# A step table for gated linear attention is written anew: order, engines and buffers' homes

## The chip, the cores and the metric

The kernel runs on one core of one Trainium2 chip. Its time is the device time of one execution in microseconds, and it is given as the median of several runs. Besides the runs there is one profiled execution, from which all rows below come. A core has a matrix engine (TensorE, PE), three engines for elementwise work (DVE, ACT and GpSimd, which the profile calls POOL), and a queue of its own (SP) from which this kernel issues all its transfers.

## The reference, cut to what matters

There are 8 batches `b`, 8 heads of 64 channels, 576 tokens and 512 channels in all.

```
q_s = softmax of q over the head's channels,   k_s = softmax of k over the tokens
kv  = einsum('bhsd,bhse->bhde', k_s, v)
x   = einsum('bhsd,bhde->bhse', q_s, kv)          # (b, 576, 512) when heads are joined
gate_pre = sum over k < 5 of conv_w[k] * x shifted by 4 - k tokens
gate = 1 / (1 + exp(-gate_pre))
val  = x @ w_val                                  # 512 x 512
out  = (gate * val) @ w_out                       # 512 x 512
```

## The kernel before

Channels lie on the partitions, in 4 blocks of 128, and tokens along the rows. So `x_b_p` is block `p` of batch `b`, 128 x 576, and the two big products, `value b m` and `project b n`, each make one block of an output from the 4 blocks of their input.

The program is a list of some 970 steps, `ORDER`. Each step is a function of the kernel with its arguments, and a last letter tells the engine where there is a choice (a is ACT, v is DVE, p is GpSimd). The steps are issued one after the other, and every engine works through its own instructions in that order. No scheduler changes it. An engine stands still when its next instruction must wait for another engine, for a transfer, or for a buffer.

Buffers come from pools with a fixed number of tiles to a tag, which are handed out in turn. A tile is reused when its last reader is done. There are 4 banks of PSUM for the results of TensorE (`bank`), 6 tiles for `gate`, 6 for staged inputs (`f`), 6 for the pairs of rounded x and its rest (`pair`), 2 for `far`, and 2 each for k, q, v, g and o.

What happens to one batch, by the names of the steps:

- `load_q`, `load_k`, `load_kc`, `load_km`, `load_qc`, `load_v`, `load_vt`, `load_kt`, `load_words` and `put` are transfers. SP issues them in the order of the list, and a load waits there until its buffer is free.
- For batches 0 and 1 q and k are worked out early and by hand: `q_max`, `q_sub`, `q_exp`, `q_each` (eight small exponentials of ACT), `q_sum`, `q_eps`, `q_rec` and `q_mul` make the softmax of q; `k_top` and `k_raise` exponentiate k by channels, and `k_turn` and `k_tail_turn` turn it on TensorE, from where `k_turned` and `k_tail_turned` copy it. `q_turn`, `tail_turn` and their copies (`q_turned`, `tail_turned`, `tail_high`) do the same for q.
- For later batches `k_peak`, `k_row`, `k_spread` and `k_sub` bring the maxima of k to its rows, and `q_total`, `q_log`, `l_turn`, `l_row`, `l_spread`, `l_sub` and `c_exp` turn the sums of q into a subtraction ahead of the exponential.
- `kv b` multiplies k and v, `kv_sums` and `kv_norm` divide by the sums, and `attend b g` makes two blocks of x, each in a bank of its own.
- `x_high` rounds a block of x, `x_low` takes the rest (on DVE), and `value` multiplies both with the rounded `w_val` and its rest: 24 products of two halves in three passes (high with low weights, high with high, low with high).
- The gate of a block starts with `first` (one tap), and 4 more follow, each either as `tap` on DVE or as `far` on ACT and `near` on GpSimd. `sigmoid` is a tanh on ACT, `gated` joins gate and val on DVE, `g_high` and `g_low` split the result, `project` multiplies it with `w_out` in the same three passes, `copy` brings a block of out to SBUF and `put` stores it.
- Blocks 0 and 1 of batch 0 take another way (`diag`, `conv_rows`, `conv_kv`, `conv`, `conv_gate`): their taps are done on TensorE.
- `field`, `part`, `scaled`, `signed` and `joined` decode a slab of weights from pairs of words, `w_high` and `w_low` split it. `taps` does the same in one step for the 20 numbers of the conv weights that each partition needs.

Every reader of `x_b_p` (`x_high`, `first`, `x_low`, `tap`, `far`) keeps its bank from the next product that shall have it.

## Time and profile before

| | |
|---|---|
| median of 3 runs | 288.62 us (288.42 to 288.87) |
| span of the profiled execution | 287.3 us |
| TensorE busy | 267.8 us, 93% of the span |
| DVE busy | 231.5 us, 81% |
| GpSimd busy | 206.2 us, 72% |
| ACT busy | 191.6 us, 67% |
| moved by DMA | 62.92 MB, 219 GB/s in the mean |

The profiled execution has a span of 287.3 us beside the 288.62 us of the median; the runs' times take in what lies around the span. Busy time is the time in which an engine has an instruction at work. Loads of weights into TensorE (PEld) run beside its products. Products are pipelined, so that one may be shown to begin before the one ahead has ended.

### The profile page before, as it was taken

How to read it: one execution, taken by the hardware profiler on the slowest of the kernel's cores; microseconds unless marked ns; L12 is line 12 of the kernel's file. 1: busy time of each engine (PE TensorE's matmuls, PEld its weight loads, DVE VectorE, ACT ScalarE, POOL GpSimd, SP SyncE). 2: the span in 40 equal slices, each digit the busy share in tenths (PEclk: the TensorE clock that was granted, in tenths of full speed). 3: DMA queues.
4: the chain of work that ended last, by engine and by line, in shares of the span. 5: the costliest groups of instructions: out<-in, count | busy, mean ns of one | idle time of the engine just before them, and what ended most of it. 6: DMA issues, size and time to landing. Idle time of an engine off the chain costs nothing.

```text
span 287.3 us, 6606 instructions
## 1 busy us (share of the span) xinstructions
PE 267.8 (93%) x2616; PEld 248.2 (86%) x2616; DVE 231.5 (81%) x332; ACT 191.6 (67%) x323; POOL 206.2 (72%) x187
## 2 busy tenths in 40 slices
PE   0198999999999999999999999999999999999995
PEld 0075799889998899889999898999989898989995
DVE  2999899999979999899669989799659774759610
ACT  2799999977797668856956773688945733645002
POOL 3767968989999986899898993879379193533300
PEclk9999999999999999999999999999999999999999
DMA  7999894598379899969997969645645700112022
GB/s 232 385 412 417 329 332 114 190 332 322 117 164 285 298 259 346 349 223 233 368 411 246 235 232 343 256 164 131 178 149 149 217 8 2 43 41 82 2 82 82
DMA packets 23462, 62.92 MB, mean 219 GB/s; under 512 B 3432, under 2 KB 3976, under 8 KB 20744
## 3 DMA queue, kind: packets, MB, share of 16 engines
q1 hardware_dynamic: 23432, 62.51, 65.5%
q8 instruction: 20, 0.33, 0.5%
q14 instruction: 10, 0.08, 0.1%
HBM read 52.96 MB, written 9.54 MB: 218 GB/s over the span
## 4 chain that ended last, share of the span: by engine, by line
PE 65%; DVE 13%; DMA 8%; POOL 6%; ACT 4%; issue 3%; SPq 0%; DVEq 0%; POOLq 0%; ACTq 0%
PE out_a L593 31%; PE val L593 25%; PE x L543 4%; DMA kc<-in_k_channels 4%; PE kv L484 3%; DMA kt<-in_k_tail 3%; POOL gl L660 2%; DVE gate L568 2%; DVE ktop L339 1%; ACT q L469 1%; DMA words<-in_w_val 1%; POOL q L471 1%; DVE g L652 1%; DVE e L263 1%; DVE qs L393 1%
## 5 line engine op out<-in xcount | busy, mean ns | idle before, releaser
L593 PE MATMUL val<-x,w_val_hi 128*128 128x288 f32 x512 | 89.0, 295 | 0.0
L568 DVE SCALAR_TENSOR_TENSOR gate<-x,cw,gate 128x575 f32<-128x575 f32 (+3 forms) x98 | 78.3, 808 | 4.8 <-ACT gate L556 1.9
L593 PEld LDWEIGHTS val<-x,w_val_hi 128*128 128x128 f32 x512 | 75.2, 188 | 0.1
L593 PE MATMUL val<-x,w_val_lo 128*128 128x288 f32 x256 | 56.0, 300 | 0.1
L593 PE MATMUL out_a<-gh,w_out_lo 128*128 128x288 f32 x248 | 54.6, 301 | 0.2 <-ACT far L573 0.2
L593 PE MATMUL out_a<-gh,w_out_hi 128*128 128x288 f32 x248 | 53.2, 296 | 0.0
L660 POOL TENSOR_TENSOR gl<-g,gh 128x576 fp32r<-128x576 f32 x25 | 36.1, 1443 | 13.8 <-ACT gh L168 6.5
L593 PEld LDWEIGHTS out_a<-gh,w_out_lo 128*128 128x128 f32 x248 | 39.3, 188 | 5.7 <-issue 2.2
L593 PE MATMUL out_a<-gl,w_out_hi 128*128 128x288 f32 x248 | 43.1, 295 | 0.3 <-POOL gl L660 0.3
L593 PEld LDWEIGHTS val<-x,w_val_lo 128*128 128x128 f32 x256 | 40.7, 188 | 1.4 <-issue 0.6
L577 POOL TENSOR_TENSOR gate<-gate,far 128x572 f32<-128x572 f32 (+3 forms) x22 | 29.0, 1320 | 16.4 <-DVE gate L568 8.1
L593 PEld LDWEIGHTS out_a<-gh,w_out_hi 128*128 128x128 f32 x248 | 39.8, 188 | 0.0
L383 POOL TENSOR_TENSOR q<-q,qm 128x512 f32<-128x512 f32 x32 | 32.9, 1044 | 6.3 <-DVE qm L378 6.3
L593 PEld LDWEIGHTS out_a<-gl,w_out_hi 128*128 128x128 f32 x248 | 36.4, 188 | 0.6 <-POOL gl L660 0.6
L174 ACT ACTIVATE o<-out_a 128x576 f32<-128x576 f32 x26 | 16.9, 651 | 29.3 <-PE out_a L593 22.6
L652 DVE SCALAR_TENSOR_TENSOR g<-gate,val 128x576 f32<-128x576 f32 x32 | 23.9, 750 | 15.4 <-PE val L593 10.1
L453 POOL TENSOR_TENSOR qc<-qc,lb 128x576 f32<-128x576 f32 (+1 forms) x17 | 24.3, 1439 | 10.8 <-DMA lb<-lrow 8.2
L318 POOL TENSOR_TENSOR k<-k,kmax 128x512 f32<-128x512 f32 x23 | 30.1, 1328 | 0.2
L580 ACT ACTIVATE gate<-gate 128x576 f32<-128x576 f32 x30 | 20.1, 682 | 8.6 <-DVE gate L568 7.1
L563 DVE TENSOR_TENSOR x<-x,x 128x576 fp32r<-128x576 f32 x32 | 23.2, 749 | 1.7 <-ACT x L168 1.6
L573 ACT ACTIVATE far<-x,cw 128x572 f32<-128x572 f32 (+3 forms) x22 | 16.2, 739 | 12.5 <-PE x L543 4.7
L168 ACT CAST x<-x 128x576 fp32r<-128x576 f32 x27 | 17.0, 640 | 7.3 <-PE x L543 4.2
(110 smaller groups left out, 441.2 us busy)
## 6 DMA issues: line engine op xcount, KB each, us to landing
out<-o SPq DMA_DIRECT2D x31, 288.0 KB, 3.9
v<-in_v SPq DMA_DIRECT2D x8, 1040.0 KB, 8.7
q<-in_q SPq DMA_DIRECT2D x7, 1024.0 KB, 8.6
km<-in_k_strided SPq DMA_DIRECT2D x24, 288.0 KB, 5.5
k<-in_k SPq DMA_DIRECT2D x6, 1024.0 KB, 8.5
qc<-in_q_channels SPq DMA_DIRECT2D x16, 288.0 KB, 7.7
lb<-lrow SPq DMA_DIRECT2D x8, 576.0 KB, 5.9
kc<-in_k_channels SPq DMA_DIRECT2D x8, 288.0 KB, 6.9
```

The lines of the kernel that those rows point to most:

```text
L168: nc.scalar.copy(out=out, in_=in_)
L174: nc.scalar.mul(out, in_, factor)
L318: engine(e).tensor_sub(kk[r, cs], kk[r, cs], mx[r, cs])
L383: engine(e).tensor_tensor(qq, qq, m, op=ALU.add if b < 2 else ALU.subtract)
L453: engine(e).tensor_sub(t, t, T["lb", b][:, p])
L563: nc.vector.tensor_sub(xl, T["x", b, p], T["xh", b, p].bitcast(F32))
L568: nc.vector.scalar_tensor_tensor(out=a, in0=x, scalar=w, in1=a, op0=ALU.mult, op1=ALU.add)
L577: nc.gpsimd.tensor_add(a, a, T["far", b, p, j])
L580: nc.scalar.activation(T["gate", b, p], T["gate", b, p], AF.Tanh, scale=0.5)
L593: nc.tensor.matmul(ps[:, cs], a[:, kb, ms], z[:, cs], start=(i == 0), stop=(i == len(parts) - 1))
L652: nc.vector.scalar_tensor_tensor(out=T["g", b, m], in0=T["gate", b, m], scalar=1.0, in1=T["val", b, m], op0=ALU.add, op1=ALU.mult)
L660: engine(e).tensor_sub(T["gl", b, m], T["g", b, m], T["gh", b, m].bitcast(F32))
```

## The change

The list of steps is another one: nearly all the same steps, in another order on all queues, 77 of them on another engine. GpSimd gives work to DVE (`g_low`, `l_sub`, `k_sub` and copies above all), and some goes between ACT and the two. `taps` becomes five steps, of which `tap_part` is now on ACT and `tap_joined` on GpSimd, so that the list grows from 967 to 971. The tags keep their number of tiles, but which tile a buffer gets is now read from a table, `HOMES`, one digit for each buffer in the order of the list.

```diff
-STAGED = 6
...
-    load_words 3, load_q 0 2 5, field 3 p, load_q 0 1 2, scaled 3 a, signed 3, load_taps, load_words 0, part 3 p,
...
+HOMES = {
+    "pair": "01234501230125340125013401250134012501",
+    "gate": "0123450213412305412305413250142035142031",
...
+    "bank": (
+        "012302302130120120102301302132101012312310202103030321302032121023021310321213201010321212102310"
+        "10213123120303012320320132"
+    ),
...
+    places = {tag: iter(order) for tag, order in HOMES.items()}
+
+    def home(pool, shape, dtype, tag, name):
+        return pool.tile(shape, dtype, tag=f"{tag}{next(places[tag])}", name=name, bufs=1)
 
     def bank(name):
-        return psum.tile([P, 2 * 512], F32, tag="bank", name=name)
-
-    def block(tag, name, bufs, dtype=F32, n=S):
-        return work.tile([P, S], dtype, tag=tag, name=name, bufs=bufs)[:, :n]
-
-    def pair(name, dtype, tag="pair", bufs=6):
-        return work.tile([P, 2 * S], dtype, tag=tag, name=name, bufs=bufs)
+        return home(psum, [P, 2 * 512], F32, "bank", name)
+
+    def block(tag, name, dtype=F32, n=S):
+        return home(work, [P, S], dtype, tag, name)[:, :n]
+
+    def pair(name, dtype, tag="pair"):
+        return home(work, [P, 2 * S], dtype, tag, name)
...
-    def taps():
-
-        w = tap_words.rearrange("p (n t) -> p n t", t=2)
-        lo, hi, e, f = w[:, :, 0].bitcast(U32), w[:, :, 1], tap_parts[:, 0], tap_parts[:, 1].bitcast(I32)
-        nc.vector.tensor_scalar(e, hi.bitcast(F32), MOST, -MOST, op0=ALU.min, op1=ALU.max)
-        nc.vector.tensor_scalar_mul(f, lo, 2.0 ** -29)
-        nc.vector.tensor_scalar_mul(e, e, 2.0 ** -112)
-        e = e.bitcast(I32)
+    def tap_field(e):
+        hi = tap_words.rearrange("p (n t) -> p n t", t=2)[:, :, 1]
+        engine(e).tensor_scalar(tap_parts[:, 0], hi.bitcast(F32), MOST, -MOST, op0=ALU.min, op1=ALU.max)
+
+    def tap_part(e):
+        lo = tap_words.rearrange("p (n t) -> p n t", t=2)[:, :, 0].bitcast(U32)
+        times(e, tap_parts[:, 1].bitcast(I32), lo, 2.0 ** -29)
+
+    def tap_scaled(e):
+        times(e, tap_parts[:, 0], tap_parts[:, 0], 2.0 ** -112)
+
+    def tap_signed():
+        hi = tap_words.rearrange("p (n t) -> p n t", t=2)[:, :, 1]
+        e = tap_parts[:, 0].bitcast(I32)
         nc.vector.tensor_scalar(e, e, 3, None, op0=ALU.logical_shift_left)
         nc.vector.scalar_tensor_tensor(e, hi, -(1 << 31), e, op0=ALU.bitwise_and, op1=ALU.bitwise_or)
-        nc.vector.tensor_add(cw_bits, e, f)
+
+    def tap_joined(e):
+        engine(e).tensor_add(cw_bits, tap_parts[:, 0].bitcast(I32), tap_parts[:, 1].bitcast(I32))
```

Three places show how the instructions move. In the rows a name with a number is a tile, `<-` stands between what is written and what is read, and the shape is that of the result.

The first place is the start of DVE's queue, before. `e` and `words` belong to the weights, `qm` are the maxima of q, `tap_words` the conv weights as they arrive and `tap_parts` their two parts, `cw` the decoded conv weights.

```order
L262 TENSOR_SCALAR e_100<-e_100 128x512
L263 SCALAR_TENSOR_TENSOR e_100<-words_95,e_100 128x512
L378 TENSOR_REDUCE qm_111<-q_97 128x8
L378 TENSOR_REDUCE qm_111<-q_97 128x16
L275 TENSOR_SCALAR tap_parts<-tap_words 128x20
L276 TENSOR_SCALAR tap_parts<-tap_words 128x20
L277 TENSOR_SCALAR tap_parts<-tap_parts 128x20
L279 TENSOR_SCALAR tap_parts<-tap_parts 128x20
L280 SCALAR_TENSOR_TENSOR tap_parts<-tap_words,tap_parts 128x20
L281 ISA cw<-tap_parts 128x40
```

And the same start of DVE's queue in the changed kernel.

```order
L302 TENSOR_SCALAR tap_parts<-tap_words 128x20
L208 TENSOR_SCALAR tap_parts<-tap_parts 128x20
L314 TENSOR_SCALAR tap_parts<-tap_parts 128x20
L315 SCALAR_TENSOR_TENSOR tap_parts<-tap_words,tap_parts 128x20
L291 TENSOR_SCALAR e_99<-e_99 128x512
L292 SCALAR_TENSOR_TENSOR e_99<-words_95,e_99 128x512
L415 TENSOR_REDUCE qm_115<-q_106 128x8
L415 TENSOR_REDUCE qm_115<-q_106 128x16
```

The decoding of the conv weights has gone ahead of the first slab of weights and of the maxima of q, and two of its six instructions have left DVE.

The second place is ACT's queue ahead of the first rounding of x (the last two rows), before. `qs` are the sums of q, `f` a part of the weights, `qT` the turned q, `qTt` its tail, `qTps` the banks that it is copied from, `x_0_1` the rounded block 1 of batch 0.

```order
L398 ACTIVATE qs_152<-qs_152 128x16
L174 ACTIVATE f_233<-words_107 128x512
L469 ACTIVATE q_97<-q_97,qs_152 128x64 x8
L168 COPY qT_252<-qTt_250 128x4x64
L174 ACTIVATE f_305<-words_144 128x512
L174 ACTIVATE f_328<-words_215 128x512
L168 COPY qT_252<-qTps_0_296 128x2x512
L168 COPY qT_252<-qTps_1_317 128x2x512
L168 CAST x_0_1_353<-x_1_342 128x576
L168 CAST x_0_0_355<-x_0_341 128x576
```

And ACT's queue ahead of the first rounding of x in the changed kernel, where `k`, `kps` and `ktz` belong to the turned k.

```order
L198 COPY k_214<-kps_1_153 128x4x256
L198 COPY ktz_83<-ktps_222 64x512
L204 ACTIVATE f_235<-words_189 128x512
L506 ACTIVATE q_106<-q_106,qs_171 128x64 x8
L198 COPY qTt_248<-qTtps_228 128x512
L204 ACTIVATE e_253<-e_253 128x512
L198 COPY qT_321<-qTt_248 128x4x64
L198 COPY qT_321<-qTps_0_301 128x2x512
L198 COPY qT_321<-qTps_1_310 128x2x512
L198 CAST w_val_hi<-f_235 128x4x128
L198 CAST x_0_1_356<-x_1_325 128x576
L198 CAST x_0_0_372<-x_0_324 128x576
```

Two parts of weights have left the stretch, and a copy of the tail of q, a scaling and the rounding of one slab of weights have come into it.

The third place is DVE's queue in the sixth batch, ahead of `attend 6 1`, before. `gate` rows are taps of blocks 0 and 1 of batch 6 (they read `x_0` or `x_1`), `x_6_0` is the `x_low` of block 0, `qc` a subtraction of batch 7 or 6, `lse` and `lt` the `l_turn` of batch 7.

```order
L170 CAST gh_3_2928<-g_3_2926 128x576
L423 TENSOR_TENSOR lse_82<-qm_2626,qs_2778 128x4x8
L428 STREAM_TRANSPOSE lt_2932<-lse_82 32x32 x4
L568 SCALAR_TENSOR_TENSOR gate_1_2970<-x_1_2917,cw,gate_1_2970 128x575
L453 TENSOR_TENSOR qc_2_2906<-qc_2_2906,lb_2710 128x576
L568 SCALAR_TENSOR_TENSOR gate_0_2976<-x_0_2916,cw,gate_0_2976 128x575
L568 SCALAR_TENSOR_TENSOR gate_0_2976<-x_0_2916,cw,gate_0_2976 128x574
L568 SCALAR_TENSOR_TENSOR gate_0_2976<-x_0_2916,cw,gate_0_2976 128x573
L563 TENSOR_TENSOR x_6_0_2972<-x_0_2916,x_6_0_2972 128x576
L568 SCALAR_TENSOR_TENSOR gate_1_2970<-x_1_2917,cw,gate_1_2970 128x574
L568 SCALAR_TENSOR_TENSOR gate_1_2970<-x_1_2917,cw,gate_1_2970 128x573
L568 SCALAR_TENSOR_TENSOR gate_1_2970<-x_1_2917,cw,gate_1_2970 128x572
```

And the same place of DVE's queue in the changed kernel, where `gl` is a `g_low` of batch 5 and `k` two `k_sub` of batch 7.

```order
L697 TENSOR_TENSOR gl_2_2914<-g_2_2871,gh_2_2912 128x576
L595 TENSOR_SCALAR gate_1_2929<-x_1_2920,cw 128x576
L605 SCALAR_TENSOR_TENSOR gate_0_2931<-x_0_2919,cw,gate_0_2931 128x574
L605 SCALAR_TENSOR_TENSOR gate_1_2929<-x_1_2920,cw,gate_1_2929 128x575
L605 SCALAR_TENSOR_TENSOR gate_1_2929<-x_1_2920,cw,gate_1_2929 128x572
L605 SCALAR_TENSOR_TENSOR gate_1_2929<-x_1_2920,cw,gate_1_2929 128x573
L605 SCALAR_TENSOR_TENSOR gate_1_2929<-x_1_2920,cw,gate_1_2929 128x574
L490 TENSOR_TENSOR qc_2_2677<-qc_2_2677,lb_2671 128x576
L605 SCALAR_TENSOR_TENSOR gate_0_2931<-x_0_2919,cw,gate_0_2931 128x575
L600 TENSOR_TENSOR x_6_0_2935<-x_0_2919,x_6_0_2935 128x576
L355 TENSOR_TENSOR k_2518<-k_2518,kmax_2882 128x512 x2
L605 SCALAR_TENSOR_TENSOR gate_0_2931<-x_0_2919,cw,gate_0_2931 128x573
```

A `g_low`, a `first`, two `k_sub` and one tap more have come into the stretch, a rounding and the `l_turn` have left it, and the last reader of `x_0`'s bank is now the last row, behind all of these.

## Rows read from the trace of the kernel before

**Rows 1.** The page, part 1: busy us (share of the span) and instructions.

```profile
PE 267.8 (93%) x2616; PEld 248.2 (86%) x2616; DVE 231.5 (81%) x332; ACT 191.6 (67%) x323; POOL 206.2 (72%) x187
```

**Rows 2.** Windows: length, busy time of each engine, clock, DMA share, GB/s.

```profile
core 0: us, PE busy (x) PEld busy (x) DVE busy (x) ACT busy (x) POOL busy (x), PEclk, DMA share, GB/s
...
2.00:25.00 23.00, 10.25 (x128) 8.11 (x128) 18.90 (x34) 16.61 (x45) 13.53 (x16) 1.00 1.01 380
...
34.00:54.00 20.00, 19.70 (x212) 18.79 (x210) 19.32 (x29) 19.21 (x48) 16.40 (x18) 1.00 0.61 188
...
95.00:103.00 8.00, 7.79 (x65) 6.93 (x66) 7.89 (x12) 6.29 (x9) 6.45 (x6) 1.00 0.84 266
...
119.00:135.00 16.00, 15.68 (x131) 14.26 (x123) 15.78 (x25) 9.47 (x15) 15.35 (x14) 1.00 0.85 249
135.00:284.00 149.00, 149.00 (x1407) 141.69 (x1405) 107.98 (x155) 85.29 (x120) 93.27 (x76) 1.00 0.50 166
```

**Rows 3.** Waits of TensorE: us in total, times, longest.

```profile
PE out_a L593 <- POOL gl L660: 0.3, 1, 0.3
PE out_a L593 <- ACT far L573: 0.2, 1, 0.2
```

**Rows 4.** Timelines, DVE and TensorE from 27 to 50: start, us, instruction.

```profile
27.01 1.42 DVE L563 TENSOR_TENSOR x<-x,x 128x576 fp32r<-128x576 f32 x2
...
32.74 0.75 DVE L563 TENSOR_TENSOR x<-x,x 128x576 fp32r<-128x576 f32 x1
...
33.64 0.37 PE L593 MATMUL val<-x,w_val_lo 128*128 128x288 f32 x1
...
49.48 1.09 PE L509 MATMUL qTps<-ident,q 128*128 128x128 f32 x8
```

**Rows 5.** Timeline of ACT at the end.

```profile
284.13 0.41 ACT L174 ACTIVATE o<-out_l 128x288 f32<-128x288 f32 x1 [1.12 <-PE out_l L593]
```

**Rows 6.** Timeline of ACT from 8 to 27.

```profile
8.59 2.02 ACT L462 ACTIVATE q<-q,qm 128x64 f32<-128x64 f32 x8 [2.94 <-DVE qm L378]
10.51 1.13 ACT L387 ACTIVATE q<-q 128x512 f32<-128x512 f32 x2
...
12.63 1.43 ACT L343 ACTIVATE kc<-kc,ktop 128x576 f32<-128x576 f32 x2
...
26.34 1.18 ACT L168 CAST x<-x 128x576 fp32r<-128x576 f32 x2 [0.42 <-PE x L543]
```

**Rows 7.** Timelines of POOL and DVE from 4 to 10.

```profile
4.35 0.63 POOL L253 TENSOR_SCALAR e<-words 128x512 f32<-128x512 f32 x1 [2.34 <-DMA words<-in_w_val]
...
5.68 0.43 DVE L262 TENSOR_SCALAR e<-e 128x512 int32<-128x512 int32 x1 [5.68 <-ACT e L174]
...
6.75 1.80 DVE L378 TENSOR_REDUCE qm<-q 128x8 f32<-128x512 f32 x2
...
8.68 1.03 DVE L277 TENSOR_SCALAR tap_parts<-tap_parts 128x20 f32<-128x20 f32 x1
```

**Rows 8.** Timeline of POOL from 32 to 34.

```profile
32.73 2.53 POOL L291 TENSOR_TENSOR w_val_lo<-f,w_val_hi 128x512 fp32r<-128x512 f32 x2
```

**Rows 9.** DMA issues: times, KB each, median us to landing.

```profile
v<-in_v SPq DMA_DIRECT2D x8, 1040.0 KB, 8.7
```

**Rows 10.** Timelines of DVE and TensorE from 178 to 224.

```profile
178.38 0.45 DVE L170 CAST gh<-g 128x576 fp32r<-128x576 f32 x1
...
203.16 0.75 DVE L652 SCALAR_TENSOR_TENSOR g<-gate,val 128x576 f32<-128x576 f32 x1
203.83 0.75 DVE L660 TENSOR_TENSOR gl<-g,gh 128x576 fp32r<-128x576 f32 x1
...
212.28 0.75 DVE L652 SCALAR_TENSOR_TENSOR g<-gate,val 128x576 f32<-128x576 f32 x1 [1.84 <-PE val L593]
...
223.00 1.20 PE L543 MATMUL x<-qT,kvd 64*64 64x288 f32 x16
```

**Rows 11.** Timeline of DVE and POOL at 266.

```profile
266.40 1.43 POOL L660 TENSOR_TENSOR gl<-g,gh 128x576 fp32r<-128x576 f32 x1
266.48 1.97 DVE L660 TENSOR_TENSOR gl<-g,gh 128x576 fp32r<-128x576 f32 x1 [0.77 <-POOL gh L170]
```

## Prediction: what the change does to the time

> **What bounds the kernel now.** I start with the page. TensorE is busy for 267.8 of the 287.3 us [rows 1], far more than any other engine, so I ask only where it is idle: that is 19.5 us. The windows give the place: from 2 to 25 us it lacks 12.75, from 34 to 54 0.30, from 95 to 103 0.21, from 119 to 135 0.32, and from 135 to 284 nothing, at a granted clock of 1.00 throughout [rows 2]; the rest is the first two and the last three microseconds. The waits name what it waited for in the middle: a product with `w_out` waited 0.3 for a `gl` of GpSimd and another 0.2 for a `far` of ACT [rows 3]. From `value 0 1` at 33.64 [rows 4] to the last product at 284.1 TensorE is a full pipe of 250.5 us. The last piece costs 0.41 for its copy [rows 5] and then its transfer, some 3.2 us in all. A different order can therefore do three things: move the 33.64, remove the 0.8 of small waits, or make new ones. The TensorE rows themselves hardly change: the same products, with the same 23 returns from a narrow product (`kv`, `attend`, `q_turn`) to a full one.
>
> The profiled execution has 287.3 us beside a median of 288.62 for the runs, so 1.3 lie around the span. I make the sum against 287.3 and carry it to 288.62.
>
> **The start.** In the kernel before, `value 0 1` waits for the DVE queue: `x_low 0 1` starts at 27.01 when ACT has rounded x, then come `x_low 0 0`, a `q_max`, four taps and `x_low 0 3`, which frees the bank at 33.49 (32.74 and 0.75), and TensorE goes on at 33.64 [rows 4]. The same seven instructions stand there in the changed order, so this piece stays 6.63 us long (33.64 less 27.01). What moves is ACT's `x_high 0 1`, at 26.34 now [rows 6]. I add up ACT's queue in the new order. An ACT instruction starts about 0.1 before the end of the one ahead, so I take differences of starts where rows have them.
>
> DVE first decodes the taps. Their words come second in the queue, right behind those that are used at 4.35; I take 4.4, and 5.0 as the other end. The tap steps cost 0.1, 1.03 (the one at 8.68, the longest of them) and 0.42, the sign steps of words 3 1.07 (5.68 to 6.75), two `q_max` 1.72: 4.4 + 4.34 = 8.8 [rows 7]. ACT's first `q_each` so starts at 8.8, 0.2 later than now (8.59). From there: `q_each` 1.92 (8.59 to 10.51), two `q_exp` 1.03, three `k_raise` at 0.68, `q_exp` 0.53, `q_each` 1.91: 16.2. The fourth `k_raise` waits for its maximum, which DVE has at about 16.55 because the block now lands as late as the vt block before: 17.25. `scaled` 0.52, `q_eps` 0.12, `k_turned` 0.90: 18.8; `k_tail_turned` can start at 18.9 and takes 0.47, `part` 0.63, `q_mul` 1.93: 21.9; `tail_turned` 0.47 (moved here from DVE), `scaled` 0.52, `tail_high` 0.29, two `q_turned` 1.80, `w_high 1` 0.52: 25.5 [rows 6]. Two parts, one scaling and a rounding step have come or gone, and the waits of this queue, as the 0.42 ahead of `x_high 0 1`, are gone. `x_high 0 1` starts at 25.5 instead of 26.34, `x_low 0 1` at 26.15, `value 0 1` at 26.15 + 6.63 = 32.8.
>
> GpSimd's `w_low 1` must be there too. It stands behind words 5, about 8.2 MB into the queue; at 380 GB/s from 2 us [rows 2] and 1.5 to 2 us more that is 25.1 to 25.6. Behind it come a `field`, a `w_high` and a `q_sub` (some 2.3), and two `joined` and two `w_low` at 1.26 [rows 8], together 7.3: 32.4 to 32.9. It does not take the lead by much. So 33.64 becomes 32.8 to 33.3; I take **-0.8**, with 0 as one end (taps late by 0.6) and -0.9 as the other.
>
> `load_v 1` now stands behind `load_km 3 0`, which waits for the `k_peak 2 3` behind `gated 0 0`, at 41 to 42 by the same sums. `kv 1` takes the place of a `q_turn` that starts at 49.48 [rows 4], so TensorE wants v at 48.7. A v load lands 8.7 us after its issue in the median [rows 9], which would be late by 1.0 to 2.0; but the queue is at 0.61 in this stretch and at 1.01 before [rows 2], so that I take 0, with 2.0 as the other end.
>
> **The middle.** The 0.21 came from an ACT `far` and the 0.32 from a GpSimd `g_low` [rows 3]. In the new order `project 1 1` takes the bank in question 1.3 us after its last reader by my count, and `g_high 2 2` is on DVE, where a cast of this kind takes 0.45 [rows 10], ahead of an idle GpSimd. I let both go: **-0.5**.
>
> The new wait that I find is `attend 6 1`. The homes put `x_6_3` into the bank of `x_6_0`, whose last reader is now `tap 6 0 1`. DVE does far more ahead of it. From the end of `value 5 0` to that of `value 5 3` TensorE needs 9.1 (`gated 5 0` at 203.16 and `gated 5 3` at 212.28 stand right behind their products). By the distances between starts in its timeline DVE has there `gated` 0.7, `q_total` 2.2, `kv_sums` and `kv_norm` 0.8, `g_high` 0.4, `g_low` 0.76, three `l_sub` 2.1, a tap 0.82, `gated` 0.7, `l_turn` 1.15: 9.6. Then, from `gated 5 3` on, TensorE needs 10.7 to `attend 6 1` (212.28 to 223.00), and DVE has `gated` 0.7, `g_low` 0.76, `first` 0.81, seven taps 5.7, `l_sub` 0.7, `x_low` 0.66, two `k_sub` 1.2: 10.5 [rows 10]. Together 20.1 of work against 19.8 less the 0.3 by which a `gated` starts behind its product. That is 0.6, and with 0.15 from a last reader to the product (33.49 to 33.64) TensorE stands still for about **+0.7**, with 0 and 1.2 as ends. Before, DVE was the one that waited here (1.84 ahead of `gated 5 3`), so nothing stood still.
>
> Elsewhere the added work on DVE (some 9 us in the whole kernel) lies in its idle time: it is busy for 108 of the 149 us from 135 to 284 [rows 2]. GpSimd loses about 19 us and waits for nobody at the end. The last pieces are swapped so that a put of 288 KB, not of 144, goes ahead of the last one; I take 0.
>
> **Sum.** -0.8 - 0.5 + 0.7 = -0.6: 286.7 in the profile, 288.0 as a median.
>
> **Rivals.** *No wait at `attend 6 1`*: if DVE keeps up there, 288.62 - 1.3 = 287.3. For it speaks that I used durations of a DVE that is often waiting.
>
> *The start stays where it is*: the tap words are a small transfer of short rows and may land at 5.0 or later; each 0.1 goes straight through to `q_each` and the whole ACT queue. Then the small gain and the new wait cancel: 288.62 - 0.5 + 0.7 = 288.8. That the new homes do nothing by themselves belongs here, since each group has as many buffers as before.
>
> *DVE and GpSimd block each other* (the slower one). One `g_low` on DVE took 1.97 instead of the 0.75 of another [rows 10], while a GpSimd `g_low` ran from 266.40 to 267.83 [rows 11]: a block costs 1.2. Instructions of DVE with two SBUF inputs (`g_low`, `l_sub`, `k_sub`) grow from 11 to 24, nine of them in the two stretches ahead of `attend 6 1`, where no room is left, so that every block there goes to the end. Two blocks give 288.0 + 2.4 = 290.4, one gives 289.2; one decides. Against it: of the 11 now, only that one shows a full block, and GpSimd has less to do.
>
> By the Trainium skill ("SBUF — State Buffer", section "Who interferes with whom") a DVE instruction with two SBUF inputs and a GpSimd instruction that reads SBUF exclude each other for a whole instruction, whichever came first; the 1.97 agrees, and by that rule any overlap among the nine would cost one of the two engines its wait.
>
> **Chances.** The forecast has 0.46, with a range of its own of 287.6 to 288.5; no wait 0.14; the start unmoved 0.17; blocks 0.23. A run can be told from no change beyond 0.2%, 0.58 us: below 288.04 or above 289.20. Of the forecast two thirds lie below 288.04, and all of the no-wait case: faster 0.46. The rest of the forecast, nearly all of the unmoved start and a little of the blocks: same 0.32. Slower 0.22. For 8 in 10 I go from 287.2 to 289.4, which leaves out the two-block case and the late `v 1` on top of it.
>
> **What would show it.** In the changed profile ACT's first `x_high` near 25.5, `val` from 32.8 on, no TensorE wait from 54 to 200, and then one of about 0.7 ahead of an `x` product near 222. Wrong would be: an `x_high` after 26, a TensorE wait on DVE of more than 1 us, `gl`, `qc` or `k` rows of DVE well above 0.76, or a wait of `kv 1` for v.

## The result: 1% slower, where the prediction expected a little faster

The changed kernel takes 291.52 us in the median of 4 runs (290.4 to 294.37), against 288.62 before: a ratio of 1.0105 (1.0062 to 1.0147). That is outside the predicted range of 287.2 to 289.4 and on the other side of no change. The profiled execution has a span of 288.6 us and a time of its own of 290.4, so it is the fastest of the four; what the other three have on top can be told only in part, below, from other executions of the same kernel. One thing to know for what follows: in every run on record the time lies 1.7 to 1.9 us above the span. The profile of before, with its span of 287.3, is thus of an execution of about 289.1 and not of one at the median. The two profiles lie 1.3 apart, the two medians 2.9.

The page of the changed kernel, part 1, shows what [rows 1] shows of before.

```profile
PE 267.7 (93%) x2616; PEld 247.8 (86%) x2616; DVE 242.0 (84%) x347; ACT 190.9 (66%) x320; POOL 191.1 (66%) x175
```

TensorE does the same 267.7 us of work. DVE has 10.5 more, GpSimd 15.1 less. The windows of [rows 2], with one more from 103 to 119, tell where TensorE now stands still.

```profile
2.00:25.00 23.00, 9.81 (x128) 7.80 (x128) 17.90 (x30) 16.39 (x43) 16.89 (x19) 1.00 0.98 372
34.00:54.00 20.00, 19.77 (x216) 19.20 (x220) 19.79 (x31) 19.52 (x45) 16.49 (x17) 1.00 0.68 248
95.00:103.00 8.00, 7.97 (x66) 6.95 (x65) 7.79 (x12) 5.56 (x9) 7.82 (x7) 1.00 0.76 213
103.00:119.00 16.00, 14.90 (x171) 14.66 (x172) 13.70 (x18) 11.64 (x15) 13.29 (x12) 1.00 0.92 289
119.00:135.00 16.00, 15.69 (x130) 13.88 (x129) 14.01 (x23) 10.77 (x17) 12.68 (x11) 1.00 0.57 181
135.00:284.00 149.00, 149.00 (x1406) 141.59 (x1405) 121.77 (x178) 82.99 (x115) 77.79 (x63) 1.00 0.55 167
```

In the new window it lacks 1.10 us. The waits of TensorE (us in total, times, longest) name the releaser. They answer to [rows 3].

```profile
PE kps L387 <- ACT kc L380: 14.9, 1, 14.9
PE val L630 <- ACT o L204: 1.1, 1, 1.1
...
PE out_a L630 <- POOL gl L697: 0.3, 1, 0.3
```

The wait for a `far` of ACT is gone, the one for a `gl` of GpSimd is still 0.3, and a `val` product now waits 1.1 for a copy of ACT. To see what each place does to the end, I compare the start of the same product in both traces. The changed one is late by 0.24 at `value 0 1` (33.88 against 33.64). It is early by 0.37 at the first `attend` of batch 1 (53.77 against 54.14): most of that is won between `value 0 1` and `k_turn 1 0`, where it takes 6.48 and before took 6.95, with a named wait of 0.2 for DVE. It loses 0.53 at `attend 2 0`, whose weights need a copy of ACT; the product behind it starts 1.66 later, where before it was 1.13:

```profile
86.20 0.39 ACT L198 COPY qT<-qTt 128x256 f32<-128x256 f32 x1
...
86.10 1.73 PE L580 MATMUL x<-qT,kvd 64*64 64x288 f32 x16
```

Before:

```profile
86.33 1.20 PE L543 MATMUL x<-qT,kvd 64*64 64x288 f32 x16
```

It is late by 0.29 at `attend 2 1` (95.18 against 94.89), wins 0.47 where before waited for a `far`, and loses 1.29 at `value 2 1`: there it is late by 1.11 (104.10 against 102.99). Behind that little is added: it is late by 1.21 at the `attend` at 119.78, by 1.29 at `attend 6 1` (224.29 against 223.00) and by 1.37 at the last copy (285.50 against 284.13 in [rows 5]). So in its fastest execution the largest loss is at one place, `value 2 1`, a second one is at `attend 2 0`, and what is won elsewhere, about 1.1, pays for that one and for the late start. These are ACT's timeline ahead of `value 2 1` and the product that waited.

```profile
97.88 0.76 ACT L593 ACTIVATE gate<-x,cw 128x576 f32<-128x576 f32 x1
99.97 0.64 ACT L198 CAST x<-x 128x576 fp32r<-128x576 f32 x1 [1.33 <-DVE gate L605]
100.51 0.41 ACT L198 COPY qT<-qTt 128x256 f32<-128x256 f32 x1
100.92 1.28 ACT L363 ACT_TABLE_LOAD   x1
102.22 0.63 ACT L363 ACTIVATE ktz<-kt 64x512 f32<-64x512 f32 x1
102.86 0.64 ACT L198 CAST x<-x 128x576 fp32r<-128x576 f32 x1
103.39 0.66 ACT L204 ACTIVATE o<-out_a 128x576 f32<-128x576 f32 x1
...
104.10 0.53 PE L630 MATMUL val<-x,w_val_lo 128*128 128x288 f32 x2 [1.14 <-ACT o L204]
```

`value 2 1` needs the bank of `project 1 2`, whose reader is `copy 1 2`, the ACTIVATE at 103.39. ACT was idle until 99.97, because `x_high 2 2` stands behind `tap 2 2 2` of DVE in the list and both read the bank of `x_2_2`. Then come a loading of ACT's function tables for 1.28 and `kt_exp 3`, which needs it, ahead of the copy. In the kernel before the copy stands ahead of the same load:

```profile
100.06 0.66 ACT L174 ACTIVATE o<-out_a 128x576 f32<-128x576 f32 x1
100.74 1.28 ACT L326 ACT_TABLE_LOAD   x1
```

The tap itself is late. Ahead of it on DVE stands the first step of `l_turn 3`, which took 0.20 before (at 94.64) and takes 0.93 here, beside a `k_sub` of GpSimd:

```profile
96.55 0.93 DVE L460 TENSOR_TENSOR lse<-qm,qs 128x32 f32<-128x32 f32 x1
...
96.11 1.29 POOL L355 TENSOR_TENSOR k<-k,kmax 128x512 f32<-128x512 f32 x1
```

An estimate from these rows: with 0.20 there, tap, cast and copy would come some 0.7 earlier, and about 0.4 of the 1.14 would be left. No run moves that step alone, so this share is not shown.

That one reader of a PSUM bank waits for another is not in the kernel's text, but in neither trace does a read of a block of x by ACT overlap with one of the same block by DVE. The Trainium skill ("PSUM — Partial Sum Buffer", section "PSUM bank collisions raise a hardware error ⚠️") says that two engines may not access one bank at the same time, reads included, and that the compiler puts a dependency between them. The 1.33, idle until the tap ended, agrees.

The start, by DVE's timeline (it answers to [rows 7]), one row of ACT ([rows 6]) and one of TensorE ([rows 4]):

```profile
4.72 0.54 DVE L302 TENSOR_SCALAR tap_parts<-tap_words 128x20 f32<-128x20 f32 x1 [4.72 <-DMA tap_words<-in_conv_w]
...
6.38 0.69 DVE L292 SCALAR_TENSOR_TENSOR e<-words,e 128x512 int32<-128x512 int32 x1
7.89 2.50 DVE L415 TENSOR_REDUCE qm<-q 128x8 f32<-128x512 f32 x3 [0.81 <-DMA q<-in_q]
...
26.57 1.73 ACT L198 CAST x<-x 128x576 fp32r<-128x576 f32 x3
...
33.88 0.50 PE L630 MATMUL val<-x,w_val_lo 128*128 128x288 f32 x2
```

The taps are decoded nearly as early as I had put it (4.72 against 4.4). But then DVE waits 0.81 for q, and everything from there is late: `q_each` starts at 9.83, not at 8.8, and `x_high 0 1` at 26.57, not at 25.5.

The place of the predicted new wait, in the timelines of DVE and TensorE ([rows 10] of before):

```profile
223.07 0.81 DVE L605 SCALAR_TENSOR_TENSOR gate<-x,cw,gate 128x573 f32<-128x573 f32 x1
...
224.29 1.20 PE L580 MATMUL x<-qT,kvd 64*64 64x288 f32 x16
```

The tap ends at 223.88 and the product starts 0.41 later, behind its own predecessor on TensorE. No wait stands there.

### The profile page after: what moved, and what is told of

Its sections match the earlier page's. It is cut to its first block, busy times and chain, and to the rows that moved or that the text cites. A ratio compares the mean times of both kernels' runs of the same rounds, so it can differ in the third digit from the quotient of the medians.

```text
span 288.6 us, 6590 instructions
## 1 busy us (share of the span) xinstructions
PE 267.7 (93%) x2616; PEld 247.8 (86%) x2616; DVE 242.0 (84%) x347; ACT 190.9 (66%) x320; POOL 191.1 (66%) x175
## 4 chain that ended last, share of the span: by engine, by line
PE 72%; DVE 12%; ACT 9%; issue 3%; DMA 2%; POOL 1%; SPq 0%; DVEq 0%; POOLq 0%
PE out_a L630 30%; PE val L630 28%; PE kv L521 5%; PE x L580 5%; DVE gate L605 4%; DMA q<-in_q 2%; ACT kc L380 1%; ACT q L506 1%; DVE x L600 1%; ACT qT L198 1%; PE kps L387 1%; PE qTps L546 1%; DVE qm L415 1%; DVE g L689 1%; POOL gl L697 1%
## 5 line engine op out<-in xcount | busy, mean ns | idle before, releaser
L697 POOL TENSOR_TENSOR gl<-g,gh 128x576 fp32r<-128x576 f32 x20 | 29.3, 1469 | 13.7 <-ACT gh L198 8.0
L204 ACT ACTIVATE o<-out_a 128x576 f32<-128x576 f32 x23 | 15.0, 651 | 22.2 <-PE out_a L630 16.5
L355 POOL TENSOR_TENSOR k<-k,kmax 128x512 f32<-128x512 f32 x21 | 27.4, 1320 | 0.1
L198 ACT CAST x<-x 128x576 fp32r<-128x576 f32 x28 | 17.6, 645 | 9.5 <-PE x L580 4.9
L415 DVE TENSOR_REDUCE qm<-q 128x8 f32<-128x512 f32 (+3 forms) x12 | 20.9, 1746 | 0.8 <-DMA q<-in_q 0.8
```

The lines of the kernel that those rows point to most:

```text
L198: nc.scalar.copy(out=out, in_=in_)
L355: engine(e).tensor_sub(kk[r, cs], kk[r, cs], mx[r, cs])
L415: nc.vector.tensor_reduce(out=T["qm", b][:, cs], in_=qq, axis=AX.X, op=ALU.max, negate=b < 2)
L697: engine(e).tensor_sub(T["gl", b, m], T["g", b, m], T["gh", b, m].bitcast(F32))
```

## The experiments

All runs of the kernel before that stand beside these have medians from 288.41 to 289.15. After each kernel I give its median, the lowest and highest run and their number, and the ratio to the kernel before with its interval where it matters. In the edits each step stands on the list as shown, and the dots are steps that stay.

### The same kernel again

No edit. The first repetition was made to see whether the 1.1 is always there, the second to have the change in the same group of runs as the mended versions at the end.

> The changed kernel as it is, to see how far its runs lie apart (290.4 to 294.37 in the first four) and what a second profile shows. All theories: a median near 291.5 us. If v 1 is what varies (theory V: load_v 1 stands behind load_km 3 0, is issued at 42.38 and has its last packet at 48.23, with kv 1 at 49.09), a profile of a longer run has kv 1 waiting at about 49 and the same distances elsewhere. If the start varies (theory S: the words of the taps and then of q land at other times), the first val moves and kv 1 with it. If the middle varies (theory M), everything up to 95 us agrees with the first profile.

Measured: 292.39 us (290.74 to 292.88, 5 runs), ratio 1.0135 (1.0114 to 1.0155). The wait at `value 2 1` is there, 1.1 at 104.26. Ahead of `attend 5 0` there is another of 0.3, behind an `l_sub 5 0` of DVE that took 1.65 instead of 0.75.

> The changed kernel once more. Theory C: if its profile is of a usual run (290.5 us of span and more), signed 2 or signed 5 takes 1.2 to 1.7 us in it and the wait ahead of conv is 1.0 or there is one of some 0.8 ahead of k_turn 1 0; if it is of a short run (288.6 to 289.0), none of these. Rival L: a usual run without long signed steps, its delay already in q_max 0 2 3.

Measured: 291.79 us (290.25 to 293.6, 10 runs), ratio 1.0075 (1.0042 to 1.0107). This profile shows a longer execution (a time of 292.37), and some of what it has on top. DVE's decoding steps and what GpSimd did beside them:

```profile
25.99 1.03 DVE L292 SCALAR_TENSOR_TENSOR e<-words,e 128x512 int32<-128x512 int32 x1
...
36.30 1.77 DVE L292 SCALAR_TENSOR_TENSOR e<-words,e 128x512 int32<-128x512 int32 x1
```

```profile
26.44 1.72 POOL L295 TENSOR_TENSOR f<-e,f 128x512 int32<-128x512 int32 x1
...
36.23 1.30 POOL L328 TENSOR_TENSOR w_val_lo<-f,w_val_hi 128x512 fp32r<-128x512 f32 x1 [1.44 <-ACT w_val_hi L198]
```

`signed 5` is 0.69 when it pays nothing and 1.77 here, where GpSimd's `w_low 2` had begun 0.07 before it. In the fastest execution of the changed kernel the two come in the other order, and it is GpSimd's step that is stretched, from 1.29 to 1.82:

```profile
35.49 0.69 DVE L292 SCALAR_TENSOR_TENSOR e<-words,e 128x512 int32<-128x512 int32 x1
...
35.52 1.82 POOL L328 TENSOR_TENSOR w_val_lo<-f,w_val_hi 128x512 fp32r<-128x512 f32 x1 [1.12 <-ACT w_val_hi L198]
```

In these two executions the one that starts later pays, DVE about 1.1 or GpSimd 0.5, and 0.03 to 0.07 us decide which. Behind DVE's step stand `k_top` and `k_turn 1 0`. From `value 0 1` to there TensorE takes 7.54 when DVE pays and 6.48 when GpSimd does. But this is not all that the longer execution has on top: of the 1.88 by which it is later at `k_turn 1 0`, 0.71 is there already behind the eight transposes of `k_turn 0 0` (19.85 against 19.14), and the stretched step at 25.99 adds some 0.1 up to `value 0 1` (34.70 against 33.88). The runs of the change lie 3 to 4 us apart; the meeting at 36 us is part of it. The longest of them, 294.37 and 293.6, also have a mean granted clock of 0.994 where the others have 0.998 to 1.00; neither was profiled, so what that adds stays open.

### Three single mendings of the changed kernel

`v_early` tests the v load of batch 1, `kt_behind` the wait of 1.1 at `value 2 1`, `taps_behind` the place of the tap words.

```diff
-    q_eps 1 0 2 p, load_vt 2, k_tail_turn 1, k_tail_turned 1 a,
...
-    load_km 3 0, k_peak 3 2, k_peak 3 1, load_v 1,
+    q_eps 1 0 2 p, load_v 1, load_vt 2, k_tail_turn 1, k_tail_turned 1 a,
...
+    load_km 3 0, k_peak 3 2, k_peak 3 1,
```

> One step moved: load_v 1 ahead of load_vt 2, where it waits for nothing (its buffer is new), so that v 1 is issued near 28 us and not 42. Theory V: the spread goes (runs within 0.5 us of each other) and the median comes to about 290.4, the best run of the change. Theories S and M: no difference beyond the spread, median 291 to 292.

Measured: 291.79 us (290.94 to 292.28, 6 runs). No effect. In the changed kernel v's last packet comes at 48.23 and `kv 1` starts at 49.09: there are 0.86 to spare. The theory that v is late falls. Its profile shows `signed 2` at 1.23 and `signed 5` at 1.67, and a wait of 0.8 ahead of `k_turn 1 0`.

```diff
-    tail_high 3 a, x_low 2 2, kt_exp 3, x_high 2 3 a,
...
-    copy 1 2 a a, q_sub 4 1 p,
+    tail_high 3 a, x_low 2 2, x_high 2 3 a,
...
+    copy 1 2 a a, kt_exp 3, q_sub 4 1 p,
```

> One step moved on ACT: kt_exp 3 (with the 1.28 us of the table load ahead of it) from in front of copy 1 2 to right behind it. In the profile of the change value 2 1 waits 1.14 us for that copy. Theory M: the wait goes and the median falls by 0.9 to 1.1 us, to about 290.5; the table load moves on behind copy 1 2, where sigmoid 2 0 and copy 1 1 may lose some 0.3 us again. Theories V and S: the wait goes too, but the spread of the runs stays as it is.

Measured: 291.95 us (290.99 to 292.96, 6 runs). The wait of 1.1 is gone from the profile: `value 2 1` starts at 103.63, 0.47 ahead of the changed kernel and 0.64 behind the kernel before, though `value 0 1` had started 0.83 later than in the change (34.71). Still the median lies within the spread of the change, and this profile shows a new wait of 0.6 and a span of 289.4:

```profile
PE x L580 <- ACT qT L493: 0.6, 1, 0.6
...
174.18 1.94 DVE L490 TENSOR_TENSOR qc<-qc,lb 128x576 f32<-128x576 f32 x1
...
174.08 1.43 POOL L490 TENSOR_TENSOR qc<-qc,lb 128x576 f32<-128x576 f32 x1
```

Two `l_sub` of one batch, one now on DVE and one on GpSimd, begin 0.10 apart; DVE's takes 1.94 instead of 0.75, and `attend 5 0` waits for it. By itself this run shows the wait removed and does not show the time won. `two_kt` below does.

```diff
-    load_words 3, load_taps, tap_field v, field 3 p, part 3 a, tap_scaled v, tap_signed, load_q 0 2 5, tap_part a,
-    tap_joined p, scaled 3 a,
...
-    q_max 0 3 5, load_q 0 1 2, q_max 0 1 2,
+    load_words 3, field 3 p, part 3 a, load_q 0 2 5, scaled 3 a,
...
+    q_max 0 3 5, load_q 0 1 2, load_taps, q_max 0 1 2, tap_field v, tap_scaled v, tap_signed,
...
```

> The load of the tap words goes behind the first q loads, as in the kernel before, and the four tap steps of DVE behind the three q_max, the one of ACT right ahead of q_each 0 4, the one of GpSimd behind q_sub 0 1. Theory S: q lands 0.4 to 0.5 us earlier, q_max 0 2 3 starts near 6.9 instead of 7.89 and q_each 0 4 near 8.7 instead of 9.83, x_high 0 1 at 26.2 or earlier instead of 26.57, median down by 0.4 to 1.0 us and a smaller spread. Rival: the ACT queue catches up before x_high 0 1 anyway (k_raise 0 1 waits for DVE at 17.3), and the median stays within 0.3 us of the change.

Measured: 292.8 us (292.57 to 293.23, 4 runs). `q_max 0 2 3` comes at 6.90 and `q_each 0 4` at 8.74, as expected: the place of the tap words costs 1.0 there. But nothing of it reaches the end. `tap_scaled` and `tap_signed`, 0.18 each in the changed kernel, take 0.96 each beside a `q_sub` of GpSimd, `k_top 0 1` comes at 17.40 instead of 16.54, and `x_low 0 1` starts at 28.94 although ACT had x rounded from 27.02 on, behind a `signed 2` of 1.66.

### Half of the list from each kernel

`head_before` has the list of before up to `kv 1` and that of the change from there; `head_after` the other way round.

> The list of the kernel before up to kv 1 (about 50 us), then what is left in the order, and on the engines, of the change; homes given anew, the change's where they are free. Theory H (most of the loss and nearly all of the spread lie in the first 50 us: q lands later behind the tap words, and the signed steps of DVE meet GpSimd): median 289.3 to 290.0, that is the kernel before and the 1.1 us wait of value 2 1, runs within 0.7 us of each other. Rival R (the rest carries it): median 291 to 292.5 with the spread of the change.

Measured: 294.75 us (294.24 to 295.05, 4 runs). The seam makes waits that neither kernel has, so that this run doesn't tell what the head is worth. The wait of 1.1 is there again, behind another head:

```profile
PE x L577 <- DVE kvd L534: 1.4, 1, 1.4
PE val L627 <- DVE g L686: 1.3, 1, 1.3
PE val L627 <- ACT o L201: 1.1, 1, 1.1
```

> The reverse: the list of the change up to kv 1, then what is left in the order of the kernel before. Theory H: median 289.8 to 291.5 with a spread of 1.5 us or more. Rival R: within 0.5 us of the kernel before, 288.3 to 289.1, and narrow.

Measured: 291.17 us (288.7 to 292.66, 8 runs), ratio 1.0075 (1.0043 to 1.0107). With the body of before the time still spreads over 4 us in 8 runs, as the change does in 4; the 19 runs of before beside it spread over 2.1. That speaks for the head as the source of most of the spread. Its median is 2.3 above that of before, so with this body the head alone costs most of what the whole change costs. Since its homes were given anew for its order, and since `two_kt` below finds 1.48 in the body, the two costs don't simply add up. In its profile `signed 1` and `signed 2` take 1.2 and `signed 5` 1.67, with a TensorE wait of 0.82 at 42.55.

### One suspect alone, in the kernel before

`taps_ahead` moves only the load of the tap words in the kernel before. `met` lets only one step of GpSimd meet a decoding step of DVE.

```diff
-    load_words 3, load_q 0 2 5, field 3 p, load_q 0 1 2, scaled 3 a, signed 3, load_taps, load_words 0,
+    load_words 3, load_taps, load_q 0 2 5, field 3 p, load_q 0 1 2, scaled 3 a, signed 3, load_words 0,
```

> The kernel before with one load moved: the tap words second in the queue, as in the change, ahead of q. Theory S (128 short rows of 160 bytes take the queue for 0.8 us and an issue of 0.44, so that q lands 1.1 to 1.3 us later): q_max 0 2 3 starts at 7.9 to 8.2 instead of 6.75, q_each 0 4 near 9.9 instead of 8.59, and the median rises by 0.6 to 1.2 us, to 289.2 to 289.9. Rival: ACT's queue has waits further on (0.45 and 0.42) that take it in, median within 0.3 us of the kernel before.

Measured: 289.84 us (288.79 to 291.8, 12 runs) against 288.85, ratio 1.0037 (1.0019 to 1.0055). One load of 20 KB, moved ahead, makes the kernel before slower by 1 us. `q_max 0 2 3` starts at 8.30 instead of 6.75, and `x_high 0 1` at 27.94 instead of 26.34. TensorE gets more than half of that back by 53 us, then loses 1.1 at another place, where an ACT `far` comes too late:

```profile
PE rows L616 <- POOL dg L608: 15.0, 1, 15.0
...
PE out_a L592 <- ACT far L572: 1.1, 1, 1.1
```

```diff
-    signed 2, joined 2 p,
...
-    q_max 1 0 2, joined 0 p, first 0 3 a,
+    signed 2, joined 0 p, joined 2 p,
...
+    q_max 1 0 2, first 0 3 a,
```

> The kernel before with one step of GpSimd moved: joined 0 ahead of joined 2, so that GpSimd works on SBUF while DVE does signed 2 (24.1 to 25.3), directly ahead of q_max 1 0 2 and x_low 0 1, which have no room. Theory C: signed 2 takes 0.5 to 1.2 us longer, x_low 0 1 starts at 27.5 to 28.2 instead of 27.01, median up by 0.3 to 1.0 us and a wider spread. Rival L: signed 2 keeps its 1.15 us and the median stays within 0.2 us of the kernel before.

Measured: 289.24 us (288.64 to 290.78, 12 runs) against 288.41, ratio 1.0032 (1.0013 to 1.005). The shift of `signed 2`, a step with one input, takes 1.48 where it took 0.42, and `x_low 0 1` starts at 28.15 instead of 27.01:

```profile
24.30 1.48 DVE L261 TENSOR_SCALAR e<-e 128x512 int32<-128x512 int32 x1
...
24.23 1.26 POOL L265 TENSOR_TENSOR f<-e,f 128x512 int32<-128x512 int32 x1
...
28.15 1.41 DVE L562 TENSOR_TENSOR x<-x,x 128x576 fp32r<-128x576 f32 x2
```

This is the meeting alone, with the kernel before around it. It shows that such a block near 25 us reaches `value 0 1`, which starts at 34.77 instead of 33.64. In the profile only 0.19 of this is left at `attend 6 1` (223.19 against 223.00), since waits that the kernel before has later take it in; the median is 0.83 higher. Where the rest of that lies isn't shown.

### Keeping the two engines apart in the changed kernel

`apart` moves `signed 2` and `joined 2` up, right behind `joined 1`, and `signed 5` and `joined 5` down, behind `k_top 1 0`. `apart_kt` has the edit of `kt_behind` as well.

```diff
-    joined 1 p, w_high 1 a, load_q 1 0 5, signed 2,
...
-    load_km 2 3, joined 2 p,
...
-    part 5 a, signed 5, joined 5 p, k_top 1 1,
...
-    k_top 1 0,
+    joined 1 p, signed 2, joined 2 p, w_high 1 a, load_q 1 0 5,
...
+    load_km 2 3,
...
+    part 5 a, k_top 1 1,
...
+    k_top 1 0, signed 5, joined 5 p,
```

> The change with two steps kept apart: GpSimd takes joined 2, which waits for signed 2 of DVE, right behind joined 1, so that it stands still while signed 2 runs; and signed 5 (with joined 5) goes behind the k_top steps of batch 1, so that a long signed 5 no longer holds up k_turn 1 0. Theory C (the longer runs, near 292.4, are those in which signed 2 and signed 5 take 1.2 to 1.7 us instead of 0.69 because GpSimd works on SBUF at the same time): signed 2 takes 1.1 in all again, no wait ahead of conv of more than 0.6 and none ahead of k_turn 1 0, median 290.4 to 291.0. Rival L (the landing of the loads alone sets the spread): median and spread as in the change, 291.5 to 292.4.

Measured: 293.64 us (293.1 to 294.13, 4 runs). Slower than the change. The second move was a mistake: it puts DVE's and GpSimd's decoding in front of what `k_turn 1 1` needs, and TensorE waits there:

```profile
PE kps L386 <- ACT ktz L197: 1.5, 1, 1.5
```

> The same, and kt_exp 3 behind copy 1 2. Theory C with the wait of value 2 1 as a part of its own: 1.0 to 1.1 us under the run before it, 289.3 to 290.0. Rival: the 1.1 us is taken up by later waits (attend 5 0 behind a long l_sub 5 0 in particular) and 0.3 to 0.6 us at most are won.

Measured: 292.61 us (291.64 to 293.43, 5 runs), 1.03 less than `apart`. This is the first time that the wait of 1.1 at `value 2 1` shows in the medians.

### The causes taken away one after the other

`two` keeps only the first move of `apart`. `two_kt` adds the edit of `kt_behind`. `mended` adds to that the tap words behind q, block 1 of k's channels ahead of words 1, and the tap steps where they meet nothing.

```diff
-    load_words 3, load_taps, tap_field v, field 3 p, part 3 a, tap_scaled v, tap_signed, load_q 0 2 5, tap_part a,
-    tap_joined p, scaled 3 a,
...
+    load_words 3, field 3 p, part 3 a, load_q 0 2 5, scaled 3 a,
...
+    load_q 0 1 2, load_taps, q_max 0 1 2, load_kc 0 0, q_each 0 4, tap_part a,
...
+    k_top 0 2, tap_field v, tap_scaled v, tap_signed, tap_joined p, diag p, k_raise 0 2,
...
-    load_words 1, load_kc 0 1,
+    load_kc 0 1, load_words 1,
```

> The change with GpSimd's joined 2 right behind joined 1, so that it waits there while signed 2 of DVE runs; signed 5 stays where it is. Theory C: signed 2 takes 1.1 us in all, x_low 0 1 starts within 0.1 of x_high 0 1's end in every profile; the part of the spread that comes from there (0.5 to 1.0 us) goes, that of signed 5 (0.8) stays: median 290.8 to 291.7. Rival L (landing of loads alone): 291.5 to 292.5 as in the change.

> The same with kt_exp 3 behind copy 1 2. If the wait of value 2 1 is a loss of its own: 0.9 to 1.2 us under the run before it, 289.8 to 290.7. If later waits take it up: within 0.4 us of it.

> The same with the first q loads ahead of the tap words, kc 0 1 ahead of words 1, and the tap steps behind the first three k_top. Theory S (q lands 1.1 us earlier and the ACT queue with it): x_high 0 1 at 25.5 to 26.0, value 0 1 at 33.0 to 33.4, median 0.4 to 1.0 us under two_kt, 289.0 to 290.0, near the kernel before. Rival: words 1 and with it w_low 1 of GpSimd come too late (33.5 or more) and nothing is won.

The medians of these three and of `again2`, all beside the same 35 runs of the kernel before (289.15):

| kernel | median us | runs | ratio to before |
|---|---|---|---|
| the change (`again2`) | 291.79 (290.25 to 293.6) | 10 | 1.0075 (1.0042 to 1.0107) |
| `two` | 291.34 (290.24 to 292.43) | 12 | 1.0064 (1.0034 to 1.0093) |
| `two_kt` | 289.86 (288.7 to 290.76) | 12 | 1.0007 (0.9978 to 1.0037) |
| `mended` | 289.58 (289.04 to 291.09) | 12 | 1.0014 (0.9989 to 1.004) |

The move of `kt_exp 3` is worth 1.48 us in the medians. In the profiles it is seen at its place: `value 2 1` starts at 104.18 behind a wait of 1.11 in `two` and at 103.19 without one in `two_kt`. The move of `signed 2` gives 0.45 and the taps 0.28; neither can be told from nothing here, and by its ratio `mended` is not ahead of `two_kt`. So two moves of single steps bring the change level with the kernel before. In `mended` `q_max` comes at 6.80 and `q_each` at 8.64, but `k_top 0 1` at 16.92, and `x_high 0 1` at 26.55 as in the change. So the early start of ACT's queue is lost again: the fourth `k_raise` waits 1.09 for the maximum, which DVE takes behind a sign step stretched to 1.02 and a reciprocal that waits for GpSimd.

### Homes alone, and one more mending

`before_homes` has the order and the engines of before, with the homes of a table. A buffer gets the home that the change gives it wherever that tile is free in the old order, and another one otherwise. The taps are decoded in single steps on DVE.

> The order and the engines of the kernel before, with buffers' homes from a table: those of the change where they are free at that place (96 of 122 banks and 28 of 38 pairs then differ from taking turns), and the conv weights decoded in single steps on DVE as before. Theory O (the order and the engines make the whole difference): within 0.4 us of the kernel before. Rival (homes): a new wait of TensorE for a bank, 0.3 us or more.

Measured: 303.51 us (301.34 to 304.65, 6 runs), ratio 1.0492 (1.0455 to 1.0529). The table made for one order, laid on another, costs 14.7 us, in waits for tiles and a lower clock behind them. The windows show the granted clock as well (it is the number ahead of the DMA share), and the row under them the longest wait:

```profile
84.50:92.00 7.50, 7.34 (x109) 7.30 (x110) 2.83 (x6) 3.90 (x6) 4.36 (x4) 0.81 0.92 198
...
98.00:104.00 6.00, 5.25 (x22) 5.25 (x23) 3.62 (x5) 1.31 (x3) 4.89 (x5) 0.50 0.62 220
...
98.75 0.85 PE L627 MATMUL out_a<-gh,w_out_lo 128*128 128x288 f32 x2 [3.92 <-DVE qT L197]
```

`mended_g` is `mended` with `g_low 2 2` on DVE, to take away the 0.3 that is left at `project 2 0`.

```diff
-    g_high 2 2 v, put 1 1,
...
-    tap 3 0 2, g_low 2 2 p, c_exp 3 3,
+    g_high 2 2 v, g_low 2 2 v, put 1 1,
...
+    tap 3 0 2, c_exp 3 3,
```

> mended with g_low 2 2 on DVE right behind g_high 2 2 instead of on GpSimd. project 2 0 waits 0.3 us for it in the change and in mended; by the rows DVE has it 0.8 us earlier, so the wait goes and the median falls by 0.2 to 0.3 us, to 0.1 to 0.4 us above or level with the kernel before. Rival: DVE is full here, and what stands behind g_low 2 2 (taps and x_low of batch 3) makes a wait of the same size.

Measured: 291.72 us (291.52 to 292.92, 6 runs), 2 more than `mended`, though in another group of runs, whose kernel before has 288.78 and not 289.15. GpSimd, free of `g_low`, begins its `k_sub` earlier, beside DVE's two steps:

```profile
122.53 1.40 DVE L199 CAST gh<-g 128x576 fp32r<-128x576 f32 x1
123.96 1.72 DVE L696 TENSOR_TENSOR gl<-g,gh 128x576 fp32r<-128x576 f32 x1
...
121.08 3.98 POOL L354 TENSOR_TENSOR k<-k,kmax 128x512 f32<-128x512 f32 x3
```

The cast took 0.46 and `g_low` 0.75 when they ran alone; the product waits 1.0 instead of 0.3. Another 1.2, at `attend 3 1`, is new too. None of the versions is shown to be shorter than the kernel before.

## Why the prediction was wrong, step by step

**The start, -0.8.** Failed, with +0.24 in its place. The step was "Their words come second in the queue [...] I take 4.4": this was right within the bounds (4.72), but I priced only the DVE work that the taps bring and not what their load does to the transfer behind it. The load takes 0.44 of issue and its 128 rows of 160 bytes pass from 3.45 to 4.24, by its packets. In my sum two `q_max` follow the sign steps without a wait. In three executions they waited 0.81, 1.22 and 0.93 for q and started at 7.89, 8.25 and 7.95; before it was 6.75, without a wait. In the fastest execution this means that `q_each` is 1.0 later than in the sum. Of this 1.0 nearly all is still there at `x_high 0 1` (26.57 against 25.5). `taps_ahead` shows the same in the kernel before, 1.6 late at `x_high 0 1`. How a load of 20 KB delays q by this much is not shown beyond these times. The 6.6 from `x_low 0 1` to `value 0 1` held (27.25 to 33.88: 6.63).

**The unmoved start as a rival.** Its mechanism, the landing of the tap words at 5.0 or later, didn't occur; its result, a start that is not earlier, did, by a mechanism that I had not looked for.

**`kv 1`, 0.** Held: `v_early` shows no effect.

**The middle, -0.5.** Half of it failed. The wait for `far` is gone. The 0.3 for `gl` is still there (0.31 at `project 2 0`): DVE's `g_high 2 2` took 0.46 and GpSimd was idle, as I had put it, but its `g_low 2 2` then takes 1.42 from 122.95 on, and the product, which could start at 124.1, waits for its end at 124.4. My sum didn't price that step. That `project 1 1` finds its bank free held, but I didn't follow the next product, `value 2 1`, whose bank hangs on `copy 1 2`. For that ACT's queue from 96 to 104 had to be added up, with the reader of DVE ahead of `x_high 2 2` and the table load in front of `kt_exp 3`. This is the largest error: 1.1 in the profile, 1.48 in the medians of `two` and `two_kt`. By the estimate above some 0.7 of the 1.1 is a block of DVE by GpSimd, so that the order of ACT's queue alone may not be the whole cause; taking `kt_exp 3` out of it is enough to remove the wait. The sum also put the rest of the stretch at nothing ("no TensorE wait from 54 to 200"), and 0.53 was lost at `attend 2 0`.

**The 1.3 around the span.** Wrong: it is 1.7 to 1.9 in every run. The profile of before is of an execution some 0.5 longer than the median. Since the forecast was made as a difference, it is not hurt by this.

**`attend 6 1`, +0.7.** Did not occur. DVE ran through as added up: from `gated 5 0` at 204.48 to the end of the tap at 223.88 it took 19.4, where I had 20.1. The sum was 0.7 too long and the wait was 0.7 long. So the rival without a wait there was right on this term.

**DVE and GpSimd block each other, 0.23 of the chances.** Right in kind and in sign, wrong in place. I looked at steps with two SBUF inputs in the stretches ahead of `attend 6 1`; the blocks behind which TensorE was seen to wait are in the weights' decoding at 25 and 36 us, on steps that stood on DVE before as well and whose neighbours on GpSimd have moved, at the step of `l_turn 3` at 96.55, and at `l_sub 5 0`. `met` shows one such block alone: +0.32% (0.13 to 0.5). Those in the decoding and at `l_sub 5 0` differ from run to run; the profile of the fastest execution shows only the one of `l_turn 3` ahead of a wait.

**Homes do nothing by themselves.** Wrong as a general sentence: `before_homes` is 14.7 us slower with as many tiles in each group. Whether the homes cost or gain anything with the order that they were made for stays open: that order with tiles handed out in turn wasn't tried.

**What adds up.** In the group of `again2` the change is 2.64 us above the kernel before, and the three moves take 2.21 of it away: 1.48 by `kt_exp 3`, 0.45 by `signed 2`, 0.28 by the taps. Only the first is clear of the spread. That early tap words and a block in the decoding cost time in the kernel before is shown by `taps_ahead` and `met`, whose intervals leave out 1; how much of the change's loss is theirs is not shown, and `head_after` says that the parts don't simply add up. The order wins some time too, 0.6 between 33.9 and 53.8 us in its fastest execution, which is part of why it can come level.

## What to carry to other kernels

When a step is moved in a queue of transfers, price the transfers that come behind it, not only the work that it feeds: a load of 20 KB in short rows made DVE 1 us late, and the whole chain of the start with it. On an engine that reads PSUM beside another one, add up its queue between two uses of each bank, with table loads in it and with the other engine's reads of the same bank as waits. And where steps of two engines stretch each other, ask of every pair of steps that the new order brings to the same time which of the two starts later, since that one is stretched; if 0.05 us decide it, runs of one kernel can differ by what the stretched step costs.

## What the runs showed of the hardware that was not expected

- Steps of DVE with a single SBUF input are stretched by GpSimd as well: a shift from 0.42 to 1.48 (`met`), a cast from 0.46 to 1.40 (`mended_g`), a step on 20 elements from 0.18 to 0.96 (`taps_behind`). I had counted only those with two inputs. The Trainium skill ("SBUF — State Buffer", section "Who interferes with whom") does name casts and `tensor_scalar` among those that can take the shared port, so these rows agree with it.
- After the wait of 3.92 in `before_homes` the granted clock was 0.50, the 1.2 GHz level, and a pair of products took 0.68 instead of 0.43. In the profiled execution of the change, with no wait above 1.1 behind the start, it was 1.00 in every window shown.
- The eight transposes of `k_turn 0 0` took 1.89 in one execution of the changed kernel (`again2`), 0.21 from one to the next, and 1.19 in another, 0.11 from one to the next, both at a granted clock of 1.00. TensorE was 0.71 late behind them. No run here tells why.
